# Rank-one pieces of an attention product as two 64-row tiles into two PSUM banks

## The chip, the cores and the metric

The kernel runs on one core of a Trainium2 chip. The metric is the device time of one execution in microseconds. Before the change it is 328.42 us, the median of three runs (328.19 to 329.14). The profile shows one execution with a span of 327.4 us and a mean granted TensorE clock of 0.986.

## The reference

A windowed attention with a few global positions feeds a token and channel mixer. There are 8 batches, 8 heads, 576 positions and 64 numbers a head.

```python
# attention: q, k, v [8, 8, 576, 64], global_idx [8]
scores = scale * np.matmul(q, k.transpose(0, 1, 3, 2))
mask = np.abs(pos[:, None] - pos[None, :]) <= 32
mask = mask | is_global[:, None] | is_global[None, :]
attn = softmax(np.where(mask, scores, -1e9))       # over the last axis
x = np.matmul(attn, v)                             # heads side by side: [8, 576, 512]
# mixer
h = np.maximum(x.transpose(0, 2, 1) @ w_tok1, 0.0) @ w_tok2
u = x + h.transpose(0, 2, 1)
out = u + np.maximum(u @ w_ch1, 0.0) @ w_ch2       # w_ch1 [512, 1536], w_ch2 [1536, 512]
```

A row of attention has three sorts of keys: those in the window, the 8 global keys, and, if the row itself is global, all keys.

## The kernel before

The positions are cut into five tiles of 128 (the last has 64). Per batch, the attention works in these steps, each a unit that is woven between the dense products of the mixer of another batch.

- **S** (line 254): scores of the window, four heads at a time as four 32-row tiles of the array; then the exponential (ScalarE, lines 263 to 269) and the mask (VectorE, line 280) into `e_all`.
- **GK** (line 295): scores of the global keys, as 32x32 tiles; their exponential and mask make `lfs`, a matrix with one row per pair of head and global key, or head and global row.
- **OG** (line 308): the sums over all keys that the global pieces need, as 32-column tiles. Its result, 128 rows by 2 x 66 columns, holds for each row the values of heads r and r + 4 (r = row // 32). VectorE makes `rf` out of it.
- **PV** (lines 328, 336, 341): the output of one tile of 128 positions. It takes `lfs` times `rf` (the rank-one pieces), and adds for each head two products of the window, 66 columns wide (64 values, the sum that the row is divided by, and one unused).

```python
def OG(b, get):
    ps = get([P, 2, 512], name=f"og_{b}")
    ...                                            # 20 products into ps[:, 0, 0:132]
    rf = mb.tile([P, H, VW], F16, tag="rf", name=f"rf_{b}")        # VW = 66
    for hg in range(2):
        nc.vector.tensor_tensor(
            out=rf[:, 4 * hg : 4 * hg + 4, :],
            in0=ps[:, 0, VW * hg : VW * hg + VW].unsqueeze(1).to_broadcast([P, 4, VW]),
            in1=dsel[:, 4 * hg : 4 * hg + 4].unsqueeze(2).to_broadcast([P, 4, VW]), op=ALU.mult,
        )

def PV(b, tau, get):
    ps = get([P, 2, 512], name=f"pv_{b}_{tau}")    # two PSUM banks
    ...
    for hf in range(2):                            # one bank for heads 0-3, one for 4-7
        nc.tensor.matmul(                          # line 328: all 128 rows of lfs and rf
            ps[:, hf, 0 : 4 * VW], lhsT=lfs[b % 2][:, QS * tau - sh : QS * tau - sh + P],
            rhs=s["rf"][:, 4 * hf : 4 * hf + 4, :], start=True, stop=False,
        )
        for hh in range(4):
            h = 4 * hf + hh
            o = ps[:, hf, VW * hh : VW * hh + VW]
            ...
            nc.tensor.matmul(o, lhsT=e_all[:, h, tau, ...], rhs=vs[:, tau, h, :], ...)         # line 336
            if tau < NT - 1:
                nc.tensor.matmul(o, lhsT=e_all[:, h, tau + 1, 0:P], rhs=vs[:, tau + 1, h, :], ...)  # line 341

    def norm():                                    # VectorE, one unit later
        pq = ps[:, :, 0 : 4 * VW].rearrange("p f (h x) -> p f h x", h=4)
        ...
        nc.vector.reciprocal(out=rr[r], in_=pq[r, :, :, D])
        nc.vector.tensor_tensor(out=x16[r, tau, :]..., in0=pq[r, :, :, 0:D], in1=rr[r]..., op=ALU.mult)
    return norm
```

`dsel` is a mask of zeros and ones: row p of `lfs` belongs to one head, and `rf` must be zero in the columns of the other seven. It comes from the row's number, in the setup:

```python
ph = int_op("ph", 4, ALU.logical_shift_right, 1, ALU.bitwise_and)       # (p >> 4) & 1
nc.vector.scalar_tensor_tensor(out=head, in0=ph, scalar=4.0, in1=p32, op0=ALU.mult, op1=ALU.add)
nc.vector.tensor_scalar(out=dsel, in0=it8, scalar1=head, scalar2=None, op0=ALU.is_equal)
```

After PV come the token products of the mixer (`M1`, line 361, with a ReLU on ScalarE at line 364; `M2`, line 377), then `u` is turned (by TensorE for batches 0 to 2, by DMA transposes from batch 3 on; the changed kernel has the same), and the channel products (line 418 with a ReLU at line 424, line 447 with the last sum at line 451), each 512 columns wide. These two lines are the dense work. The order, with the units of one batch woven into the dense work of the batch before:

```python
for b in range(B):
    D4, D5 = dense(b)                              # lines 418 and 447 of batch b
    ...
    merge(A, D4)                                   # A: OG, five PV steps, M1 of batch b + 1
    merge(Bs, D5)                                  # Bs: M2 of batch b + 1, S and GK of batch b + 2
```

In the first batch there is no dense work yet, and dummy products (line 103) stand between the units.

Of the kernel before, what the change touches and what calls it, by code (L numbers as in the profile page):

```python
# [8 lines left out]
F32 = mybir.dt.float32  # L9
F16 = mybir.dt.float16  # L10
I32 = mybir.dt.int32
AF = mybir.ActivationFunctionType
ALU = mybir.AluOpType
# [4 lines left out]
P = 128  # L18
NT = 5
NG = 8  # L20
WIN = 32
QS = P + NG
EW = 2 * P + NG
VW = 66
# [8 lines left out]
def kernel(  # L33
# [12 lines left out]
    nc = tc.nc  # L46
    B, H, S, D = q.shape
# [9 lines left out]
    const = ctx.enter_context(tc.tile_pool(name="const", bufs=1))  # L57
    stg = ctx.enter_context(tc.tile_pool(name="stg", bufs=1))
    mb = ctx.enter_context(tc.tile_pool(name="mb", bufs=2))
    ob = ctx.enter_context(tc.tile_pool(name="ob", bufs=3))  # L60
    tiny = ctx.enter_context(tc.tile_pool(name="tiny", bufs=4))
# [85 lines left out]
    def iota(shape, dtype, pattern, base=0, mult=0, name=None):  # L147
        t = const.tile(shape, dtype, name=name)
        nc.gpsimd.iota(t, pattern=pattern, base=base, channel_multiplier=mult, allow_small_or_imprecise_dtypes=True)
        return t  # L150

    def int_op(name, s1, op, s2=None, op2=None):
        t = const.tile([P, 1], I32, name=name + "_i")
        nc.vector.tensor_scalar(out=t, in0=pi_i, scalar1=s1, scalar2=s2, op0=op, **({"op1": op2} if op2 else {}))  # L154
        f = const.tile([P, 1], F32, name=name)
        nc.vector.tensor_copy(out=f, in_=t)
        return f
# [9 lines left out]
    lfs = [const.tile([P, NT * QS], F16, name=f"lf{i}") for i in range(2)]  # L167
# [11 lines left out]
    gkT = const.tile([P, 2, 2, 32], I32, name="gkT")  # L179
    idx_i = const.tile([P, 4], I32)  # L180
    bandm = const.tile([P, NT, 200], F16)
    dsel = const.tile([P, H], F32)
    mf = const.tile([P, LW], F16)

    def gather(g, ten, bh):
# [118 lines left out]
    def OG(b, get):  # L304
        ps = get([P, 2, 512], name=f"og_{b}")
        for c in range(NT):
            for r in range(4):
                nc.tensor.matmul(
                    ps[32 * r : 32 * r + 32, 0, 0 : 2 * VW].rearrange("p (g x) -> p g x", g=2), lhsT=egs[b % 2][:, c, r],
                    rhs=vsh[b % 2][:, c, r::4, :], start=(c == 0), stop=(c == NT - 1),  # L310
                )
        rf = mb.tile([P, H, VW], F16, tag="rf", name=f"rf_{b}")
        for hg in range(2):
            nc.vector.tensor_tensor(
                out=rf[:, 4 * hg : 4 * hg + 4, :],
                in0=ps[:, 0, VW * hg : VW * hg + VW].unsqueeze(1).to_broadcast([P, 4, VW]),
                in1=dsel[:, 4 * hg : 4 * hg + 4].unsqueeze(2).to_broadcast([P, 4, VW]), op=ALU.mult,
            )
        st[b]["rf"] = rf

    def PV(b, tau, get):
        s = st[b]
        ps = get([P, 2, 512], name=f"pv_{b}_{tau}")
        odd_last = tau == NT - 1 and b % 2 == 1
        sh = 64 if odd_last else 0
        x16, vs = x16s[b % 2], vsh[b % 2]
        for hf in range(2):
            nc.tensor.matmul(  # L328
                ps[:, hf, 0 : 4 * VW], lhsT=lfs[b % 2][:, QS * tau - sh : QS * tau - sh + P],
                rhs=s["rf"][:, 4 * hf : 4 * hf + 4, :], start=True, stop=False,  # L330
            )
            for hh in range(4):
                h = 4 * hf + hh
                o = ps[:, hf, VW * hh : VW * hh + VW]
                last = hh == 3
                nc.tensor.matmul(  # L336
                    o, lhsT=e_all[:, h, tau, QS - sh : QS - sh + P], rhs=vs[:, tau, h, :],
                    start=False, stop=last and tau == NT - 1,
                )
                if tau < NT - 1:  # L340
                    nc.tensor.matmul(o, lhsT=e_all[:, h, tau + 1, 0:P], rhs=vs[:, tau + 1, h, :], start=False, stop=last)  # L341

        def norm():
            r = slice(0, P) if tau < NT - 1 else slice(sh, sh + 64)
            pq = ps[:, :, 0 : 4 * VW].rearrange("p f (h x) -> p f h x", h=4)
            rr = tiny.tile([P, 2, 4], F32, tag="rr", name=f"rr_{b}_{tau}")
            nc.vector.reciprocal(out=rr[r], in_=pq[r, :, :, D])  # L347
            nc.vector.tensor_tensor(  # L348
                out=x16[r, tau, :].rearrange("p (f h x) -> p f h x", f=2, h=4), in0=pq[r, :, :, 0:D],
                in1=rr[r].unsqueeze(3).to_broadcast([P if tau < NT - 1 else 64, 2, 4, D]), op=ALU.mult,  # L350
            )
        return norm

# [150 lines left out]
    def u_PV(b, tau, get):  # L504
        def f():
            norm = PV(b, tau, get)
            later(LAG_PV, norm)
        return f
# [4 lines left out]
    def phase_og(b):  # L513
        return [(0.3, lambda: OG(b, pss))] + [(0.8, u_PV(b, t, psv if t % 2 else pss)) for t in range(NT)]
# [66 lines left out]
    it8 = iota([P, NG], F32, [[1, NG]], name="it8")  # L581
# [19 lines left out]
    p32 = int_op("p32", 5, ALU.logical_shift_right)  # L601
# [14 lines left out]
        nc.vector.memset(kTs[i].bitcast(F16)[:, :, 2 * (WIN + S) :], 0.0)  # L616
    nc.vector.memset(w1l, 0.0)
    nc.vector.memset(w2[:, :, S:], 0.0)
    ph = int_op("ph", 4, ALU.logical_shift_right, 1, ALU.bitwise_and)
    hi8 = int_op("hi8", 3, ALU.logical_shift_right, 1, ALU.bitwise_and)  # L620
    head = const.tile([P, 1], F32)
    nc.vector.scalar_tensor_tensor(out=head, in0=ph, scalar=4.0, in1=p32, op0=ALU.mult, op1=ALU.add)
    nc.vector.tensor_scalar(out=dsel, in0=it8, scalar1=head, scalar2=None, op0=ALU.is_equal)
    nc.vector.memset(mf, 0.0)
    for i in range(2):
        nc.vector.memset(lfs[i][:, LW:], 0.0)
# [16 lines left out]
        out=ohk, in0=gidx_f.unsqueeze(1).to_broadcast([P, NT, NG]),  # L643
        in1=kpos.unsqueeze(2).to_broadcast([P, NT, NG]), op=ALU.is_equal,
# [12 lines left out]
    for hg in range(2):  # L657
# [9 lines left out]
        out=bandm, in0=band.unsqueeze(1).to_broadcast([P, NT, 200]),  # L667
        in1=rowok.unsqueeze(2).to_broadcast([P, NT, 200]), op=ALU.mult,
# [12 lines left out]
    def eg_const(i):  # L681
# [21 lines left out]
        out=mf[:, 0 : 4 * QS].rearrange("p (t x) -> p t x", x=QS)[:, :, 0:P],  # L703
        in0=it_f[:, 0 : 4 * P].rearrange("p (t x) -> p t x", x=P),
        scalar1=gpp, scalar2=hi8, op0=ALU.is_equal, op1=ALU.max,
# [148 lines left out]
```

The softmax here doesn't subtract the row's maximum and nothing guards it: scores larger than these inputs give would overflow.

## Time and profile before

| What | Value |
|---|---|
| Time, median of 3 | 328.42 us |
| TensorE busy | 308.2 us, 94% of the span |
| VectorE busy | 186.5 us, 57% |
| ScalarE busy | 158.0 us, 48% |
| GpSimd busy | 75.3 us, 23% |
| Dense products, lines 418 and 447 | 92.9 and 92.5 us |
| PV, lines 328, 336, 341 | 21.7, 27.6 and 23.4 us |
| `rf` on VectorE, line 314 | 16 instructions, 427 ns each |
| Division after PV, line 348 | 40 instructions, 691 ns each |
| HBM traffic | 36.12 MB read, 9.44 MB written |

Engines have short names: PE is TensorE's products, PEld its weight loads, DVE is VectorE, ACT ScalarE, POOL GpSimd, SP the queue that issues most transfers. A line of a group gives the source line, the engine and operation, output and input by name, the shapes and the count; then the busy time and the mean time of one, and then how long the engine was idle just before and what ended that. For TensorE the shape begins with the rows and columns of the array in use, as in 128\*128 or 32\*128. A product's own duration includes the pipeline behind it, and durations of successive products overlap.

### The profile page before, as it was taken

The numbers are of one execution on the slowest core, as the hardware profiler recorded it, in microseconds if no ns is written. First come the engines' busy times: TensorE is split into PE (matmuls) and PEld (weight loads), VectorE is DVE, ScalarE is ACT, GpSimd is POOL, SyncE is SP. The second block draws the span as 40 slices with busy tenths as digits, with TensorE's granted clock in tenths as the row PEclk, the third lists the DMA queues.
The fourth block names the chain that finished last, engine by engine and source line by source line (L and its number), as shares of the span: only waits on it lengthen the run. The fifth ranks groups of instructions, "written<-read, shape, count | busy, mean of one in ns | idle before, by whom it ended". The sixth has DMA issues, their size and how long they took to land.

```text
span 327.4 us, 7329 instructions
## 1 busy us (share of the span) xinstructions
PE 308.2 (94%) x3000; PEld 156.3 (48%) x3000; DVE 186.5 (57%) x348; ACT 158.0 (48%) x295; POOL 75.3 (23%) x154
## 2 busy tenths in 40 slices
PE   6499998989899999999999999999999999999994
PEld 2236443635366444644466445544565446444641
DVE  7698677658657476826671476537572655151021
ACT  5482585123955383457544564448453454404600
POOL 5794260164071014201420014101400000000000
PEclk9689999999999999999999999999999999999998
DMA  7999969999999969914891559025101320043012
GB/s 157 181 243 231 189 109 164 252 151 280 237 207 244 166 191 254 204 34 107 255 221 33 128 157 212 20 64 115 36 2 27 103 83 16 2 110 98 2 71 89
DMA packets 67893, 44.55 MB, mean 136 GB/s; under 512 B 53140, under 2 KB 59156, under 8 KB 67860
## 3 DMA queue, kind: packets, MB, share of 16 engines
q1 hardware_dynamic: 62292, 39.60, 52.4%
q0 software_dynamic: 5568, 4.49, 9.1%
q8 instruction: 23, 0.38, 0.5%
q14 instruction: 10, 0.08, 0.1%
HBM read 36.12 MB, written 9.44 MB: 139 GB/s over the span
## 4 chain that ended last, share of the span: by engine, by line
PE 71%; DMA 14%; DVE 4%; SPq 4%; ACT 3%; POOL 2%; issue 1%; POOLq 0%; DVEq 0%; ACTq 0%
PE op L447 26%; PE b1p L418 21%; DMA q<-in_q_dram 7%; PE hp L377 5%; DMA v<-in_v_dram 4%; PE a1p L361 4%; PE s L254 4%; PE b1lp L434 3%; SPq L95 2%; DMA wc<-in_moe_w_ch_dram 2%; PE pv L336 2%; DVE e_all L280 2%; PE pv L328 2%; PE pv L341 2%; PE gk L295 1%
## 5 line engine op out<-in xcount | busy, mean ns | idle before, releaser
L418 PE MATMUL b1p<-uT,wc 128*128 128x512 f16 x384 | 92.9, 379 | 2.0 <-DVE b L422 0.9
L447 PE MATMUL op<-wc,b 128*128 128x512 f16 x384 | 92.5, 379 | 0.0
L424 ACT ACTIVATE b<-b1p 128x512 f16<-128x512 f32 x90 | 53.9, 599 | 61.7 <-PE b1p L418 61.3
L447 PEld LDWEIGHTS <-b 128*128 128x128 f16 x384 | 35.4, 98 | 41.8 <-issue 4.2
L418 PEld LDWEIGHTS <-wc 128*128 128x128 f16 x384 | 34.2, 97 | 39.8 <-issue 5.5
L280 DVE TENSOR_TENSOR e_all<-e_all,bandm 128x1000 f16<-128x1000 f16 x64 | 42.3, 722 | 15.2 <-ACT e_all L269 15.1
L451 DVE TENSOR_TENSOR osb<-u,op 128x512 f32<-128x512 f16 x32 | 21.9, 685 | 36.0 <-PE op L447 33.9
L382 DVE TENSOR_TENSOR u<-x,hp 128x1024 f16<-128x1024 f16 x14 | 17.1, 1221 | 42.4 <-PE hp L377 42.4
L263 ACT ACTIVATE e_all<-s 128x800 f16<-128x800 f32 x32 | 25.2, 841 | 29.1 <-PE s L254 28.9
L283 POOL COPY eg<-e_all 128x160 f16<-128x160 f16 x14 | 4.6, 331 | 136.4 <-DVE e_all L280 103.0
L348 DVE TENSOR_TENSOR x<-pv,rr 128x512 f16<-128x512 f32 (+1 forms) x40 | 27.6, 691 | 1.5
L145 POOL CAST k<-k 128x576 f16<-128x576 f32 x28 | 18.7, 699 | 40.2 <-DVE rr L347 17.4
L336 PE MATMUL pv<-vsh,e_all 128*128 128x66 f16 x320 | 27.6, 193 | 0.0
L254 PE MATMUL s<-qT,kT 32*128 32x200 f16 (+1 forms) x640 | 20.8, 244 | 6.9 <-DVE qT L203 4.4
L336 PEld LDWEIGHTS <-e_all 128*128 128x128 f16 x320 | 24.0, 98 | 4.8
L198 POOL CAST vsh<-v 128x512 f16<-128x512 f32 x38 | 23.4, 656 | 10.1 <-DMA v<-in_v_dram 10.1
L141 ACT CAST q<-q 128x576 f16<-128x576 f32 x28 | 18.4, 685 | 14.9 <-DMA q<-in_q_dram 14.6
L341 PE MATMUL pv<-vsh,e_all 128*128 128x66 f16 x256 | 23.4, 193 | 0.0
L103 PE MATMUL w<-zz 128*128 128x512 f16 x66 | 21.3, 438 | 1.3 <-DVE p_i L154 1.3
L254 PEld LDWEIGHTS <-kT 32*128 32x128 f16 x640 | 11.9, 95 | 22.2 <-issue 18.3
L328 PE MATMUL pv<-rf,lf 128*128 128x264 f16 x80 | 21.7, 275 | 0.0
L377 PE MATMUL hp<-a,w 128*128 128x512 f16 x72 | 19.3, 379 | 1.9 <-ACT a L364 1.5
(134 smaller groups left out, 333.1 us busy)
## 6 DMA issues: line engine op xcount, KB each, us to landing
q<-in_q_dram SPq DMA_DIRECT2D x64, 128.0 KB
out_dram<-osb SPq DMA_DIRECT2D x32, 256.0 KB
k<-in_k_dram SPq DMA_DIRECT2D x14, 576.0 KB
v<-in_v_dram SPq DMA_DIRECT2D x24, 256.0 KB
v<-in_v_dram SPq DMA_DIRECT2D x16, 192.0 KB
wc<-in_moe_w_ch_dram POOLq DMA_DIRECT2D x6, 512.0 KB, 10.2
q<-in_q_dram SPq DMA_DIRECT2D x16, 64.0 KB
out_dram<-osb SPq DMA_DIRECT2D x8, 128.0 KB
```

Of the source, the lines that this page charges most:

```text
L198: (nc.scalar.copy if eng else nc.gpsimd.tensor_copy)(out=vsh[b % 2][:, c, :, 0:D], in_=n32v[b % 2][:, c])
L254: nc.tensor.matmul(tiles[r // 2][:, r % 2, off : off + n], lhsT=kT[rs, P * c : P * c + P, e], rhs=qf[rs, lo : lo + n, e], start=(e == 0), ...
L263: nc.scalar.activation(out=e2[:, :, 1:3, 64:EW], in_=ps[:, :, 0:400].rearrange("p h (c x) -> p h c x", c=2), func=AF.Exp, scale=scale)
L280: nc.vector.tensor_mul(out=eh, in0=eh, in1=bandm)
L328: nc.tensor.matmul(ps[:, hf, 0 : 4 * VW], lhsT=lfs[b % 2][:, QS * tau - sh : QS * tau - sh + P], rhs=s["rf"][:, 4 * hf : 4 * hf + 4, :], s ...
L336: nc.tensor.matmul(o, lhsT=e_all[:, h, tau, QS - sh : QS - sh + P], rhs=vs[:, tau, h, :], start=False, stop=last and tau == NT - 1,)
L341: nc.tensor.matmul(o, lhsT=e_all[:, h, tau + 1, 0:P], rhs=vs[:, tau + 1, h, :], start=False, stop=last)
L348: nc.vector.tensor_tensor(out=x16[r, tau, :].rearrange("p (f h x) -> p f h x", f=2, h=4), in0=pq[r, :, :, 0:D], in1=rr[r].unsqueeze(3).to_ ...
L377: nc.tensor.matmul(ps[:, i, :], lhsT=w2[:, ch, P * tau - sh : P * tau - sh + P], rhs=s["a1"][:, ch, :], start=(ch == 0), stop=(ch == 1),)
L418: nc.tensor.matmul(ps, lhsT=wc1[:, cc, P * j : P * j + P], rhs=s["uT"][:, :, cc, :], start=(cc == 0), stop=(cc == 3))
L424: nc.scalar.activation(out=s["b1"][:, j, :], in_=ps, func=AF.Relu)
L447: nc.tensor.matmul(ps, lhsT=w, rhs=wc2[:, j, :], start=(j == 0), stop=(j == NJ - 1))
```

## The change

The 128 rows of `lfs` and `rf` are four groups of 32 by r, the head modulo 4. Rows 0 to 63 concern only heads with r of 0 or 1, rows 64 to 127 only those with r of 2 or 3. So the columns are put in another order: bank 0 gets the heads with r of 0 and 1, bank 1 those with r of 2 and 3. Then each bank's rank-one product needs only 64 of the 128 rows, and the two become 64-row tiles of the array with a bank each, which may run at once. `rf` shrinks to half, since each row keeps just the four heads of its half, and one VectorE instruction makes it. The window's products go through the heads in the new order, and the division reads PSUM in it. The purpose is to have the second rank-one product run beside the first.

```diff
-    dsel = const.tile([P, H], F32)
+    dsel = const.tile([P, 4], F32)
...
-        rf = mb.tile([P, H, VW], F16, tag="rf", name=f"rf_{b}")
-        for hg in range(2):
-            nc.vector.tensor_tensor(
-                out=rf[:, 4 * hg : 4 * hg + 4, :],
-                in0=ps[:, 0, VW * hg : VW * hg + VW].unsqueeze(1).to_broadcast([P, 4, VW]),
-                in1=dsel[:, 4 * hg : 4 * hg + 4].unsqueeze(2).to_broadcast([P, 4, VW]), op=ALU.mult,
-            )
+        rf = mb.tile([P, 2, 2, VW], F16, tag="rf", name=f"rf_{b}")
+        nc.vector.tensor_tensor(
+            out=rf, in0=ps[:, 0, 0 : 2 * VW].rearrange("p (g x) -> p g x", g=2).unsqueeze(1).to_broadcast([P, 2, 2, VW]),
+            in1=dsel.rearrange("p (r g) -> p r g", r=2).unsqueeze(3).to_broadcast([P, 2, 2, VW]), op=ALU.mult,
+        )
...
+        pr = ps.rearrange("p f (r x) -> p (f r) x", r=2)
         for hf in range(2):
+            rs = slice(64 * hf, 64 * hf + 64)
             nc.tensor.matmul(
-                ps[:, hf, 0 : 4 * VW], lhsT=lfs[b % 2][:, QS * tau - sh : QS * tau - sh + P],
-                rhs=s["rf"][:, 4 * hf : 4 * hf + 4, :], start=True, stop=False,
-            )
-            for hh in range(4):
-                h = 4 * hf + hh
-                o = ps[:, hf, VW * hh : VW * hh + VW]
-                last = hh == 3
+                pr[:, 2 * hf : 2 * hf + 2, 0 : 2 * VW], lhsT=lfs[b % 2][rs, QS * tau - sh : QS * tau - sh + P],
+                rhs=s["rf"][rs].rearrange("p r g x -> p r (g x)"), start=True, stop=False,
+            )
+        for r in range(4):
+            for g in range(2):
+                h = 4 * g + r
+                o = pr[:, r, VW * g : VW * g + VW]
+                last = r % 2 == 1 and g == 1
...
-            pq = ps[:, :, 0 : 4 * VW].rearrange("p f (h x) -> p f h x", h=4)
-            rr = tiny.tile([P, 2, 4], F32, tag="rr", name=f"rr_{b}_{tau}")
-            nc.vector.reciprocal(out=rr[r], in_=pq[r, :, :, D])
+            pq = pr[r, :, 0 : 2 * VW].rearrange("p r (g x) -> p r g x", g=2)
+            rr = tiny.tile([P, 4, 2], F32, tag="rr", name=f"rr_{b}_{tau}")
+            nc.vector.reciprocal(out=rr[r], in_=pq[:, :, :, D])
             nc.vector.tensor_tensor(
-                out=x16[r, tau, :].rearrange("p (f h x) -> p f h x", f=2, h=4), in0=pq[r, :, :, 0:D],
...
+                out=x16[r, tau, :].rearrange("p (g r x) -> p r g x", g=2, r=4), in0=pq[:, :, :, 0:D],
...
-    ph = int_op("ph", 4, ALU.logical_shift_right, 1, ALU.bitwise_and)
+    ph = int_op("ph", 4, ALU.logical_shift_right, 3, ALU.bitwise_and)
...
-    head = const.tile([P, 1], F32)
-    nc.vector.scalar_tensor_tensor(out=head, in0=ph, scalar=4.0, in1=p32, op0=ALU.mult, op1=ALU.add)
-    nc.vector.tensor_scalar(out=dsel, in0=it8, scalar1=head, scalar2=None, op0=ALU.is_equal)
+    nc.vector.tensor_scalar(out=dsel, in0=it8[:, 0:4], scalar1=ph, scalar2=None, op0=ALU.is_equal)
```

More of the change, by code (lines that the diff above doesn't have):

```diff
@@ L344, in norm @@
             r = slice(0, P) if tau < NT - 1 else slice(sh, sh + 64)
-            pq = ps[:, :, 0 : 4 * VW].rearrange("p f (h x) -> p f h x", h=4)
-            rr = tiny.tile([P, 2, 4], F32, tag="rr", name=f"rr_{b}_{tau}")
-            nc.vector.reciprocal(out=rr[r], in_=pq[r, :, :, D])
+            n = P if tau < NT - 1 else 64
+            pq = pr[r, :, 0 : 2 * VW].rearrange("p r (g x) -> p r g x", g=2)
+            rr = tiny.tile([P, 4, 2], F32, tag="rr", name=f"rr_{b}_{tau}")
+            nc.vector.reciprocal(out=rr[r], in_=pq[:, :, :, D])
             nc.vector.tensor_tensor(
-                out=x16[r, tau, :].rearrange("p (f h x) -> p f h x", f=2, h=4), in0=pq[r, :, :, 0:D],
-                in1=rr[r].unsqueeze(3).to_broadcast([P if tau < NT - 1 else 64, 2, 4, D]), op=ALU.mult,
+                out=x16[r, tau, :].rearrange("p (g r x) -> p r g x", g=2, r=4), in0=pq[:, :, :, 0:D],
+                in1=rr[r].unsqueeze(3).to_broadcast([n, 4, 2, D]), op=ALU.mult,
             )
```

## The prediction

> **What bounds the kernel now.** I read the page first: busy shares, the chain that ended last, then the groups of instructions.
>
> ```profile
> PE 308.2 (94%) x3000; PEld 156.3 (48%) x3000; DVE 186.5 (57%) x348; ACT 158.0 (48%) x295; POOL 75.3 (23%) x154
> ...
> PE 71%; DMA 14%; DVE 4%; SPq 4%; ACT 3%; POOL 2%; issue 1%; POOLq 0%; DVEq 0%; ACTq 0%
> ...
> L336 PE MATMUL pv<-vsh,e_all 128*128 128x66 f16 x320 | 27.6, 193 | 0.0
> ...
> L341 PE MATMUL pv<-vsh,e_all 128*128 128x66 f16 x256 | 23.4, 193 | 0.0
> ...
> L328 PE MATMUL pv<-rf,lf 128*128 128x264 f16 x80 | 21.7, 275 | 0.0
> ```
>
> TensorE is busy 94% of the span and carries 71% of the chain. The three lines that the change touches (328, 336, 341) have no idle time before them. The printed 275 ns is not what a product costs: matmuls are pipelined, so the cost is the distance from one start to the next. That stands in the timeline of TensorE alone, here around one PV step (columns: start, time until the last one ends, what, how many):
>
> ```profile
> 200.33 0.28 PE L328 MATMUL pv<-rf,lf 128*128 128x264 f16 x1
> 200.44 0.19 PE L336 MATMUL pv<-vsh,e_all 128*128 128x66 f16 x1
> 200.47 0.20 PE L341 MATMUL pv<-vsh,e_all 128*128 128x66 f16 x1
> ...
> 200.66 0.19 PE L341 MATMUL pv<-vsh,e_all 128*128 128x66 f16 x1
> 200.69 0.27 PE L328 MATMUL pv<-rf,lf 128*128 128x264 f16 x1
> 200.80 0.19 PE L336 MATMUL pv<-vsh,e_all 128*128 128x66 f16 x1
> ...
> 201.04 1.02 PE L418 MATMUL b1p<-uT,wc 128*128 128x512 f16 x4
> 201.91 0.28 PE L328 MATMUL pv<-rf,lf 128*128 128x264 f16 x1
> ```
>
> A rank-one product (264 columns) costs 0.11 us, a small one 0.03, a 512-column one 0.216 (four in 0.87). In nanoseconds, over the whole trace, the steps are 112, 29 to 35, and 216: 0.42 ns a column. A whole PV step of 18 products takes 712 ns on average; the last one of a batch, with 10 products, 482.
>
> The kernel already changes the shape of the array elsewhere. The scores (line 254) use 32-row tiles and the global sums (line 308) 32-column tiles, both between full-size products. Two more stretches of the same timeline:
>
> ```profile
> 151.02 0.81 PE L447 MATMUL op<-wc,b 128*128 128x512 f16 x3
> 151.77 0.54 PE L254 MATMUL s<-qT,kT 32*128 32x200 f16 x16
> 152.24 0.61 PE L447 MATMUL op<-wc,b 128*128 128x512 f16 x2
> ```
>
> ```profile
> 127.69 0.38 PE L418 MATMUL b1p<-uT,wc 128*128 128x512 f16 x1
> 128.00 0.47 PE L308 MATMUL og<-vsh,eg 128*32 128x132 f16 x20
> 128.40 0.39 PE L418 MATMUL b1p<-uT,wc 128*128 128x512 f16 x1
> ```
>
> Three 512-column products should occupy 0.65 us before the scores start, but they take 0.75; one should occupy 0.22 before line 308, but takes 0.31. From the single starts: full to 32 rows 312 ns instead of 216 (+96), full to 32 columns 309 (+93). On the way back, the last 200-column score to the first full product is 176 ns, where 200 columns are worth 84 (+92); the last 132-column one is 151, where 56 would do (+95). The step after that first full product is 226 instead of 216 (+10). These figures repeat within 3 ns at nearly every such place from 90 us on. So one visit to another array shape costs 96 + 92 + 10, some 198 ns.
>
> Last, where PV steps don't count. From the timeline of all engines at the end of batch 1:
>
> ```profile
> 69.16 1.46 PE L447 MATMUL op<-wc,b 128*128 128x512 f16 x6
> ...
> 70.13 1.46 ACT L141 CAST q<-q 128x576 f16<-128x576 f32 x2 [5.29 <-DMA q<-in_q_dram]
> ...
> 71.50 1.08 ACT L364 ACTIVATE a<-a1p 128x512 f16<-128x512 f32 x2
> 72.14 1.08 PE L377 MATMUL hp<-a,w 128*128 128x512 f16 x3 [1.53 <-ACT a L364]
> ```
>
> ScalarE waits for a q load, then does the ReLU that TensorE waits for: 1.53 us of TensorE idle, put there by a transfer. Traced in order of time, the chain up to 70.9 us consists of transfers and their issue. The PV steps of batches 0 and 1 (at 28 to 32 and 60 to 66 us) lie before this wait, and delay nothing as long as they grow by less than it.
>
> **What the Trainium skill says.** "TensorEngine Tiling (Array Packing)", Tiling Modes, Key Properties: changing the tiling mode, as against the tile, drains TensorE. The trace agrees: +96 and +92 ns at each change above. "TensorE: Matmul & The Clock Gate", Part 3 (Packing small matmuls): products in different row groups run at once and start about 4 ns apart. The trace agrees: the four 32-row tiles of a score group start 3 to 4 ns apart. "TensorEngine Tiling (Array Packing)", Restrictions and Gotchas, Gotcha 1: different row tiles can't use one PSUM bank at the same time. The change gives each half its own bank. No run so far has 64-row tiles; I take their cost from the 32-row ones.
>
> **The change part by part.**
>
> *Order.* The issue order moves on TensorE only inside a PV step: the two line-328 products now stand together at its head, then the 16 (or 8) small ones. Counts are equal: 80 and 576. On VectorE it loses eight rf multiplies and one setup instruction. Nothing moves between engines.
>
> *The pair.* Before, 2 x 112 = 224 ns. After, each has 64 rows and still 264 columns: the first starts, the second 4 ns later, and both are done 112 ns on: 116 ns. Saved: 108 ns a step.
>
> *The shape changes.* Before, a PV step had 128x128 products alone, between 128x128 products. After, it enters 64-row mode (+96), leaves it (+92), and the step after that is 10 longer: +198 ns.
>
> *Sum.* 198 - 108 = +90 ns for each of 40 steps. 30 of them (batches 2 to 7, 91 to 278 us) lie among products that follow each other without a gap: 30 x 0.090 = +2.7 us. The other 10 add 0.9 us ahead of the 1.53 us wait, and vanish in it.
>
> *VectorE.* One rf multiply a batch goes (427 ns each, 8 x 0.427 = 3.4 us of busy time). TensorE never waits for rf: line 328 has 0.0 idle before it, because full-size products are put between the global sums and the first PV step. Worth 0. The division after PV reads the same 512 elements in another order, four dimensions as before; I keep its 691 ns.
>
> *Setup.* The instruction that made `head` goes from VectorE's queue. It began at 4.68 us and its follower at 4.86, so 0.18 us, and the queue leads to the first gather on the chain. The transfers behind it are limited by throughput, so I count -0.1.
>
> Total: 328.4 + 2.7 - 0.1 = 331.0 us, +0.8%.
>
> **The rivals.**
>
> *No drain for 64 rows*, because the weights of the next shape load beside the running product. Then only the gain is left: 30 x 0.108 = 3.2 us, 325.1 us. For it: it is what the change is for. Against it: both kinds of shape change in the trace pay it each time, rows or columns, one way and the other.
>
> *Drain and no overlap*: the pair runs one after the other. Then 30 x 0.198 = +5.9 us, 334.2 us. Against it: the score groups overlap four at a time.
>
> *The growth hides elsewhere, or is passed on.* If waits at batch boundaries (0.2 to 0.7 us each, for VectorE and ScalarE, 1.1 in all after 90 us) swallow some: 330. If the division grows by its new reading order, the token product after it would wait; 0.1 us for each of six batches is +0.6, 331.6.
>
> **Range and chances.** The middle case rests on repeated numbers of this trace, and the extrapolation from 32 to 64 rows is its weak point. A tail without the +10 gives 330.7; a shape change 20 ns cheaper each way 329.8; one 20 dearer 332.2. So 329.7 to 332.2. Both rivals stay within 2% (321.9 to 335.0), so "within" gets 0.95; slower by over 2% needs no overlap and a further loss: 0.03; faster by over 2% needs more than the whole gain: 0.02.
>
> **What would show it.** In the timeline after: about 0.31 us from the start of the last full product to the first rank-one product, the second within 5 ns, then 0.20 us to the first small product; a PV step of about 0.71 us from its first product, plus 0.10 ahead of it. A 0.22 us approach would mean that the first rival is right. Two products 0.11 apart mean the second. The wait of 1.53 us for the ReLU should shrink to about 0.7. The prediction fails if the 64-row shape costs nothing to enter, or if that wait is not there to absorb batches 0 and 1 (+0.9).

## The result, and the profile after

The changed kernel takes 332.24 us, the median of four runs (331.46 to 332.70), beside 328.60 for the kernel before. The ratio is 1.0107, with a 95% interval of 1.008 to 1.0134: slower by about one per cent. The prediction was 331.0, with a range of 329.7 to 332.2, so the median lies at the upper end of the range. As a growth over the kernel before, it is 3.6 us where 2.6 was predicted, with a range of 1.3 to 3.8. The span of the profile grew from 327.4 to 330.2 us.

From the page after, the busy shares and the chain, and from the groups with shapes kept apart, PV's and `rf`'s lines (328 to 342 are PV, 313 makes `rf`, 350 divides), with the weight loads of line 328 in the kernel before as the last row:

```profile
PE 312.5 (95%) x3000; PEld 149.4 (45%) x3000; DVE 184.3 (56%) x339; ACT 157.8 (48%) x295; POOL 75.1 (23%) x154
...
PE 71%; DMA 14%; DVE 4%; SPq 4%; ACT 3%; POOL 2%; issue 1%; ACTq 0%; POOLq 0%; DVEq 0%
```

```profile
L337 PE MATMUL pv<-vsh,e_all 128*128 128x66 f16 x320 | 23.3, 194 | 0.0
L350 DVE TENSOR_TENSOR x<-pv,rr 128x512 f16<-128x512 f32 x32 | 22.1, 691 | 1.2
L342 PE MATMUL pv<-vsh,e_all 128*128 128x66 f16 x256 | 19.8, 193 | 0.0
...
L328 PE MATMUL pv<-rf,lf 64*128 64x264 f16 x80 | 11.4, 283 | 0.0
...
L328 PEld LDWEIGHTS <-lf 64*128 64x128 f16 x80 | 3.8, 92 | 16.2 <-issue 11.3 <-DVE rf L313 3.0 <-DVE rr L349 1.3
...
L313 DVE TENSOR_TENSOR rf<-og,dsel 128x264 f16<-128x264 f32 x8 | 3.5, 433 | 13.0 <-PE og L308 13.0
```

```profile
L328 PEld LDWEIGHTS <-lf 128*128 128x128 f16 x80 | 7.7, 97 | 4.4 <-DVE x L348 0.2
```

Read by busy time, the change is a success: line 328 fell from 21.7 to 11.4 us, the two lines of small products from 51.0 to 43.1. None of that is time. The busy time counts an instant once, however many products overlap in it, and more of them overlap now. What is new is the 16.2 us of idle before the weight loads of line 328, where it was 4.4. Of this, 11.3 is "issue", which means that they waited for nothing that the profile shows. The weight loads for the 64-row shape do not start ahead: at the step below the first one starts at 201.74 us, together with its product and 308 ns after the start of the last full-size product. Before the change (a step at 201.91 us) it starts 2 ns after the start of that product and 0.21 us ahead of its own. The profile puts 3.0 us of that idle time down to `rf`, in seven places, but the distance from the last full-size product to the first 64-row one is 309 to 312 ns in all 40 steps, so `rf` delays none of them. The timeline of TensorE at one PV step:

```profile
201.00 0.81 PE L420 MATMUL b1p<-uT,wc 128*128 128x512 f16 x3
201.74 0.28 PE L328 MATMUL pv<-rf,lf 64*128 64x264 f16 x2
201.96 0.20 PE L337 MATMUL pv<-vsh,e_all 128*128 128x66 f16 x1
202.00 0.20 PE L342 MATMUL pv<-vsh,e_all 128*128 128x66 f16 x1
202.03 0.19 PE L337 MATMUL pv<-vsh,e_all 128*128 128x66 f16 x1
...
202.46 1.02 PE L420 MATMUL b1p<-uT,wc 128*128 128x512 f16 x4
```

From the first of three 512-column products to the pair it is 0.74 us, where 0.65 would do. The pair is one row, "x2", since the second starts 3 ns after the first. Then come 0.22 us to the first small product, and 0.04 to the next where 0.03 was usual. The gain is there, and each side of it has lost about a tenth of a microsecond.

Laid over each other by the starts of the same products, the two traces show where the 2.75 us come from. At 74 to 91 us the changed kernel is 0.13 ahead. Each batch from 2 to 7 then adds 0.48, all of it in its PV steps: 0.36 behind after the first, 0.84, 1.32, 1.79, 2.28, 2.75 after the last. Batches 0 and 1 leave nothing, as these rows of all engines at the end of batch 1 show:

```profile
69.94 1.46 PE L449 MATMUL op<-wc,b 128*128 128x512 f16 x6
70.11 1.35 ACT L141 CAST q<-q 128x576 f16<-128x576 f32 x2 [5.37 <-DMA q<-in_q_dram]
...
71.37 1.08 ACT L366 ACTIVATE a<-a1p 128x512 f16<-128x512 f32 x2
...
72.01 1.29 PE L379 MATMUL hp<-a,w 128*128 128x512 f16 x4 [0.62 <-ACT a L366]
```

TensorE comes to the wait 0.78 us later than before and waits 0.62 us in place of 1.53; the product behind it starts at 72.01, where it was 72.14.

### The profile page after: what moved, and what is told of

It reads as the page before. It is cut to its first block, busy times and chain, and to the rows that moved or that the text cites. A ratio compares the mean times of both kernels' runs of the same rounds, so it can differ in the third digit from the quotient of the medians.

```text
span 330.2 us, 7320 instructions
## 1 busy us (share of the span) xinstructions
PE 312.5 (95%) x3000; PEld 149.4 (45%) x3000; DVE 184.3 (56%) x339; ACT 157.8 (48%) x295; POOL 75.1 (23%) x154
## 4 chain that ended last, share of the span: by engine, by line
PE 71%; DMA 14%; DVE 4%; SPq 4%; ACT 3%; POOL 2%; issue 1%; ACTq 0%; POOLq 0%; DVEq 0%
PE op L449 25%; PE b1p L420 21%; DMA q<-in_q_dram 7%; PE hp L379 5%; DMA v<-in_v_dram 4%; PE a1p L363 4%; PE s L254 4%; PE b1lp L436 3%; PE pv L337 3%; SPq L95 3%; DMA wc<-in_moe_w_ch_dram 2%; DVE e_all L280 2%; PE pv L328 2%; PE pv L342 2%; PE gk L295 1%
## 5 line engine op out<-in xcount | busy, mean ns | idle before, releaser
L337 PE MATMUL pv<-vsh,e_all 128*128 128x66 f16 x320 | 23.3, 194 | 0.0
L337 PEld LDWEIGHTS <-e_all 128*128 128x128 f16 x320 | 18.6, 97 | 4.9
L267 ACT ACTIVATE e_all<-s 128x272 f16<-128x272 f32 x32 | 13.0, 408 | 15.5 <-PE s L254 15.2
L217 DVE STREAM_TRANSPOSE kT<-k 128x576 int32<-128x576 int32 x16 | 19.9, 1244 | 0.3 <-DMA k<-in_k_dram 0.3
```

The lines of the kernel that those rows point to most:

```text
L337: nc.tensor.matmul(o, lhsT=e_all[:, h, tau, QS - sh : QS - sh + P], rhs=vs[:, tau, h, :], start=False, stop=last and tau == NT - 1,)
```

## The experiments

Theory: changing the array's shape twice a PV step costs more than the overlap brings. A visit is one such change to 64-row tiles and the change back. Main rival: the new order of heads, banks and division costs, not the shape. Times below are medians against the kernel before in runs beside them on the same chip.

### The full rows again, in the new order

```diff
-        rf = mb.tile([P, 2, 2, VW], ...)      # four heads a row
+        rf = mb.tile([P, 4, 2, VW], ...)      # eight heads a row, with zeros
...
-            rs = slice(64 * hf, 64 * hf + 64)
+            rs = slice(0, P)
...
-                rhs=s["rf"][rs].rearrange(...)
+                rhs=s["rf"][rs, 2 * hf : 2 * hf + 2].rearrange(...)
```

> The changed kernel with its new order of heads, banks and division, but the rank-one products on all 128 rows again (rf has its zeros back). Theory (the change of array shape is what costs): no step of PV changes shape, a step takes 712 ns and follows the dense product by 216, and the time is that of the kernel before, 328.4 us give or take 0.5 (ratio 0.998 to 1.001). Rival (the new order of banks and heads, or the division that reads it, is what costs): it stays slow, 331.5 us or more. Beside that: if the output in two runs of 132 columns is what made the step from the pair to the first small product 215 ns where I had 204, the step from a 128-row product to the first small one is now about 123 ns; if it is the 64-row shape, it stays 112.

Measured: 328.59 us, ratio 1.0006 (0.9983 to 1.0029). TensorE's timeline at the same step:

```profile
200.84 1.04 PE L420 MATMUL b1p<-uT,wc 128*128 128x512 f16 x4
201.72 0.38 PE L328 MATMUL pv<-rf,lf 128*128 128x264 f16 x2
201.94 0.19 PE L337 MATMUL pv<-vsh,e_all 128*128 128x66 f16 x1
201.97 0.19 PE L342 MATMUL pv<-vsh,e_all 128*128 128x66 f16 x1
```

The two rank-one products follow each other at 112 ns, 224 in all, and the dense product ahead keeps its 216 ns (222 ahead of the first step of most batches). A PV step of 18 products takes 709 ns on average (712 before), the last one of a batch 469 (482 before). The new order costs nothing, and even saves a little, so the rival falls. The output in two runs of 132 columns costs nothing either: the step from the second rank-one product to the first small one is 112 ns, as before.

### Two visits to the 64-row shape in a step

```diff
-        for hf in range(2):
-            (64-row product of bank hf)
         for r in range(4):
+            if r % 2 == 0:
+                hf = r // 2
+                (64-row product of bank hf)
             for g in range(2):
```

> The changed kernel, but the second 64-row product stands ahead of its own bank's small products: two visits to the 64-row shape in a PV step, and nothing runs at once. Theory (a visit costs 96 on the way in, 103 on the way out and 10 after, about 210 ns): a PV step grows by some 420 ns over the kernel before, 30 steps give +12.6 us, and batches 0 and 1 give 4.2 us less the 1.5 us wait: about 343.5 us (342 to 345). Rival (the order of banks and the division cost, the visits are nearly free): 332 to 335 us, the 0.1 us of lost overlap a step.

Measured: 342.74 us, ratio 1.0436 (1.0398 to 1.0474). In TensorE's timeline the second visit lies between small products:

```profile
209.71 0.28 PE L330 MATMUL pv<-rf,lf 64*128 64x264 f16 x1
209.92 0.20 PE L338 MATMUL pv<-vsh,e_all 128*128 128x66 f16 x1
...
210.14 0.19 PE L343 MATMUL pv<-vsh,e_all 128*128 128x66 f16 x1
210.27 0.28 PE L330 MATMUL pv<-rf,lf 64*128 64x264 f16 x1
210.48 0.20 PE L338 MATMUL pv<-vsh,e_all 128*128 128x66 f16 x1
```

From the last small product to the second 64-row one it is 124 ns on average, where small products otherwise follow at 29: the entry costs 95 ns after a 66-column product as after a 512-column one (311 in place of 216). A PV step of 18 products is 416 ns longer than before, 208 for each visit, and the time lies in the range that the theory gave.

### The tiles in batches 0 and 1 alone

```diff
-            rs = slice(0, P)
+            rs = slice(64 * hf, 64 * hf + 64) if b < 2 else slice(0, P)
```

> The full-row version, with the two 64-row tiles in batches 0 and 1 alone (10 of the 40 PV steps). Theory (their growth vanishes in the wait for a transfer): TensorE's wait for the ReLU shrinks from 1.5 us to about 0.6, and the time is 328.4 us, equal to the full-row version within 0.3. Rival (all 40 steps count): 10 x 0.097 = 1.0 us more, 329.4 us.

Measured: 328.12 us, ratio 0.9987 (0.9967 to 1.0006), against 1.0006 for the full-row version. Ten longer steps add nothing that the median shows; 329.4 us is excluded. The trace shows something else than was expected: the wait for the ReLU did not shrink to 0.6 us but is gone altogether, since the transfer came earlier in this execution, the fastest of the 14 (ScalarE's cast of q starts at 69.0 us, before at 70.1). From batch 3 on the distance to the kernel before stays as it is (1.9 us ahead at 138 us, 2.0 at 320). That the median lies a little under the full-row version's has a likely reason in the clocks on record: eight of the 22 full-row runs had a mean granted clock of 0.984 or less and a median of 330.2 us, the other 14 a median of 328.4; here no run was so low.

### Fewer visits

```diff
-        ps = get([P, 2, 512], name=f"pv_{b}_{tau}")
+        for t in {0: (0, 1, 2), 3: (3, 4)}.get(tau, ()):
+            s["pv", t] = (psv if t % 2 else pss)([P, 2, 512], ...)
+            (both 64-row products of t)
+        ps = s["pv", tau]
```

> The changed kernel with the same 64-row pairs, but those of position tiles 0, 1 and 2 stand together, and those of 3 and 4: two visits a batch in place of five. Theory (the cost is per visit): a visit of three pairs is 96 + 2 x 115 + 218 + 11 = 555 ns where the kernel before spends 6 x 112 = 672, one of two pairs 440 against 448: 0.125 us a batch gained, six batches 0.75, and 0.1 of the setup: 327.6 us, some 0.2% under the kernel before (ratio 0.996 to 0.9995). Rival (the cost is per pair, whatever stands beside it): 331.5 us or more, as in the changed kernel.

Measured: 329.67 us, ratio 1.0028 (1.0005 to 1.0052): better than the changed kernel, but not under the kernel before, where I expected it. In the dense part it does what was expected. TensorE's timeline, with three pairs in one row:

```profile
201.01 0.59 PE L424 MATMUL b1p<-uT,wc 128*128 128x512 f16 x2
201.54 0.51 PE L330 MATMUL pv<-rf,lf 64*128 64x264 f16 x6
201.98 0.20 PE L341 MATMUL pv<-vsh,e_all 128*128 128x66 f16 x1
```

Three pairs take 0.44 us where six full-size products took 0.67. From 120 us (1.41 behind) to 290 us (0.65 behind) the trace gains 0.15 us a batch on the kernel before. What it lost, it lost ahead of that. TensorE arrives 0.34 us earlier at the wait for the transfer, so it idles longer, 1.74 us. Then this:

```profile
72.02 1.34 PE L383 MATMUL hp<-a,w 128*128 128x512 f16 x4 [1.74 <-ACT a L370]
73.16 1.48 PE L453 MATMUL op<-wc,b 128*128 128x512 f16 x3
74.43 1.91 PE L383 MATMUL hp<-a,w 128*128 128x512 f16 x4
```

Four products of 512 columns that should end in 1.03 us take 1.91; from 73.2 us on, eight steps are 421 to 427 ns instead of 216. The table by stages says why, here for this kernel (stretch, its length, then busy time of each engine; the granted clock is the number before the last two):

```profile
66.00:70.00 4.00, 4.00 (x20) 1.85 (x19) 3.30 (x6) 0.19 (x1) 2.98 (x7) 1.00 1.24 145
70.00:74.00 4.00, 2.14 (x8) 0.68 (x6) 1.29 (x2) 2.14 (x4) 3.09 (x4) 0.89 1.04 188
74.00:78.00 4.00, 4.00 (x14) 1.60 (x13) 2.20 (x3) 0.00 (x0) 2.59 (x5) 0.68 1.09 317
```

and for the kernel before, which idles 1.53 us there:

```profile
74.00:78.00 4.00, 4.00 (x32) 2.28 (x31) 3.45 (x5) 0.00 (x0) 2.98 (x6) 1.00 1.16 317
```

After the longer idle time TensorE is granted 0.68 of its clock in this stretch and does 14 products in it, where the kernel before did 32 (16 of them short ones, of 128 columns). At the same product the kernel is 0.12 us ahead of the kernel before at 72 us and 1.57 behind at 75. The trace of the full-row version has the same, after 2.06 us idle (six steps of 427 ns); those of the kernel before (1.53) and of the changed kernel (0.62) have none. The clocks of the other runs go the same way: 14 of the 22 grouped runs had a mean clock of 0.984 or less, with a median of 329.97 us, and the other eight a median of 328.14. Of 51 runs of the kernel before, ten were so low, with 330.5 us beside 328.3. My expectation had left this out.

### Grouped from batch 2 on

```diff
-        for t in {0: (0, 1, 2), 3: (3, 4)}.get(tau, ()):
+        for t in ({0: (0, 1, 2), 3: (3, 4)} if b > 1 else {i: (i,) for i in range(NT)}).get(tau, ()):
```

> The grouped pairs (three, then two) from batch 2 on, and single pairs, as in the changed kernel, in batches 0 and 1. Theory (grouping gains 0.15 us a batch in the dense part; what the grouped kernel lost, it lost at 70 to 78 us, where TensorE arrived early, idled 1.7 us for a transfer and then ran for some 3 us at about half its clock): TensorE arrives late again, idles under 1 us, keeps its clock, and the time is that of the kernel with tiles in batches 0 and 1 alone less 6 x 0.15: 327.2 us, ratio to the kernel before 0.994 to 0.998. Rival (grouping itself costs, as its 1.0028 says): 329 us or more.

Measured: 328.54 us, ratio 0.9982 (0.9959 to 1.0005). The mechanism is as expected: idle 1.2 us, clock 1.00 throughout, and in the dense part from 0.11 us behind the kernel before to 0.81 ahead. The median is 1.3 us above what I expected. Runs of one kernel scatter by a microsecond or two, and at 72 us the traces stand anywhere from 1.1 us ahead of the kernel before (tiles in batches 0 and 1) to 0.7 behind (full rows). The interval holds both a gain of 0.4% and none: inconclusive on the time.

### Dummy products in the wait

```diff
-            merge(... + X_units(2)[:2] + phase_m(1)[:5] + ..., D5)
+            merge(... + X_units(2)[:2] + zero(lambda: fill(8)) + phase_m(1)[:5] + ..., D5)
```

> All batches grouped, and eight dummy products of 512 columns (1.7 us) in TensorE's queue ahead of batch 1's second token product, where it waits for a transfer. They compute nothing that is used. Theory (the clock falls because of that wait): the wait becomes work, the products at 72 to 76 us keep steps of 216 ns in place of 427, and the time falls from 329.7 to 327.9 us (327.2 to 328.4). Rival (the transfer alone sets it, or the grouping): 329.5 us or more.

Measured: 327.58 us, ratio 0.9964 (0.9947 to 0.9982), the one version of this study that beats both kernels. TensorE's timeline at the place of the wait:

```profile
69.12 1.89 PE L103 MATMUL w<-zz 128*128 128x512 f16 x8
70.85 0.81 PE L453 MATMUL op<-wc,b 128*128 128x512 f16 x3
71.49 1.03 PE L383 MATMUL hp<-a,w 128*128 128x512 f16 x4
```

No idle time, and four products in 1.03 us again. None of 22 runs took 329.9 us or more; of the 22 without the dummies, eight did. One of these 22 had a clock of 0.984 or less, where 14 had without the dummies.

> The kernel before with the same eight dummy products in the same place, as the control of the last one. Theory: its wait of 1.5 us mostly did not cost it the clock, so the median stays at 328.3 us (327.9 to 328.6, ratio 0.997 to 1.001), with fewer runs at 330 and over. Rival (dummies bring something in themselves): 327.5 us or less.

Measured, the same line in the kernel before: 328.43 us, ratio 0.999 (0.9976 to 1.0005). Five of its 22 runs had a clock of 0.984 or less too, so this mark doesn't stand for the wait alone. By themselves the dummies bring next to nothing, so the gain of the grouped version over this control, 328.43 - 327.58 = 0.85 us, fits the grouping: six batches by 0.15 are 0.9. In three traces (all grouped, grouped late, grouped with dummies) the dense part shows these 0.15. In the time the gain showed in one version of two: the one grouped from batch 2 on, with the same six batches, is not below this control (328.54).

### The changed kernel without the wait

The same line in the changed kernel.

> The changed kernel with the eight dummy products that the kernel before got in the control (328.43 us there), so that nothing is left of the wait in which the growth of batches 0 and 1 vanished. They compute nothing that is used. Theory (each PV step grows by 97 ns wherever it stands, and the wait alone hid ten of them): all 40 steps count, 328.4 + 40 x 0.095 - 0.1 = 332.1 us (331.6 to 332.7). Rival (the transfers of the opening set that point with or without dummies, so ten steps stay hidden): 328.4 + 2.9 - 0.1 = 331.2 us (330.8 to 331.5).

Measured: 331.94 us, ratio 1.0122 (1.0103 to 1.0141), inside the theory's range and above the rival's. The trace agrees in part. Batch 1's 0.48 us counts: 0.03 behind the kernel before ahead of those PV steps, 0.51 after them. Batch 0's does not show: the trace is 0.38 us behind ahead of another wait, at 50 us (for a ReLU on VectorE, 0.9 us in the kernel before, 0.6 here), and 0.03 behind after it. I had not seen this wait. It differs from trace to trace (0.9 us in the changed kernel, none in the control), so what it hides is not settled, nor how many of the ten steps come out. Nor do the times show that the wait for the ReLU hid anything in the changed kernel, which loses 3.64 us to the kernel before without the dummies (332.24 - 328.60) and 3.65 with them (331.94 - 328.29).

## Why the prediction held, step by step

*The entry, +96 ns*, and *no idle time ahead of PV before*: right. Entering 64-row mode costs 95 ns on average (311 from start to start, mean of all 40 steps), where the figure taken from the 32-row scores was 96. The entries measured here lie between 93 ns (32 columns) and 96 (32 rows), after 66-column and 512-column products alike.

*The pair, 116 ns in place of 224, and the exit, +92*: right in kind, 10 ns short in size. The step from the second product to the first small one is 215 ns, and 112 + 92 is 204. The grouped kernel shows where the missing 10 belong. There the step from the first pair to the second is 120 and to the third 109 ns, and the exit after the last pair is 205, as predicted. So it isn't the exit. The first product in a new shape runs some 10 ns longer, on the way in as well as on the way out. I had put that on the way out alone (*+10*), where it showed: the next small product comes after 39 ns instead of 29. The trace of the kernel before had it on the way in too: among 32-row scores of 200 columns the fifth product starts 92 to 94 ns after the fourth, the ninth 76 to 81 after the eighth.

*The sum, +90 ns a step*: measured, +98 in steps of 18 products and +86 in the last of a batch, some 477 ns a batch where I had 450. Six batches are 2.9 us in place of 2.7. That this is so close is in part luck: the missing 10 ns a step were partly made up for by the new order, which saves 3 ns in a step of 18 products and 13 in the last (the full-row version), and which the sum left out too.

*Batches 0 and 1 vanish in the wait*: right in the traces of the two kernels, where the wait shrank from 1.53 to 0.62 us, and tiles in those batches alone cost nothing. The medians do not show it: 3.6 us is nearer to what all 40 steps would cost, 8 x 0.477 = 3.8, than to 2.9, and the interval of the ratio (2.6 to 4.4 us) holds both.

*VectorE, worth 0*: right. The division stayed at 691 ns and `rf` at 433 an instruction, half as many. *Setup, -0.1*: the traces have the changed kernel 0.13 ahead at 74 us. Other things scatter as much there, so it isn't shown to be the setup.

*The rivals*: no drain for 64 rows would have brought a 0.22 us approach; it is 0.31. No overlap would have set the pair 0.11 apart; it is 0.003. The new reading order costs nothing, which the full-row version shows directly. The waits at batch boundaries after 90 us hid nothing: they are 0.69 us at 126 us and 0.17 to 0.23 at four other places, in both traces.

What is left: 331.0 was predicted and 332.24 measured. About 0.2 of that is the 10 ns. The profiled runs of the two kernels differ by 2.74 us (331.88 and 329.14), as their traces do; the medians differ by 3.6. The rest is scatter, and what sets it in these two kernels is not shown. The wait at 50 us, for one, differs from trace to trace, and the one of 0.69 us at 126 us stands in five of the ten traces of this study and is missing in the others.

## What to carry to other kernels

Splitting a product into row tiles that run at once pays only if the time saved in one visit exceeds two changes of shape: here 209 ns a visit, against 108 saved by a pair of 264 columns, so a second pair in the same visit makes it even, and a third makes it a gain. Before adding a shape, measure the step from start to start across a change that the kernel already has; it gave this result to within 8 ns a step. And read the distance between starts, not the busy time, which fell on all three lines of PV. Four 32-row tiles at once were not tried.

## What was not expected of the hardware

- The first product after a change of shape takes about 10 ns more than its columns are worth, in either direction: 120 instead of 109 to 112 for 264 columns on the way into 64-row tiles, 226 instead of 216 for 512 columns on the way out of the scores.
- Idle time of 1.7 and 2.1 us in the middle of the kernel was followed by six to eight products at half speed (427 ns for 512 columns), some 3 us at a granted clock of 0.50, while 1.5, 1.2 and 0.6 us were not. So in the grouped kernel TensorE reached a wait 0.34 us sooner and was later behind it. Each of these is one trace, and no more than these five lengths were measured.
